# Seven block products for the first layer of both halves of a second MLP, with its last weights converted early and parked in DRAM

## The chip, the cores and the metric

One core of one Trainium2 chip runs the whole program in one launch. The metric is the device time of an execution in microseconds (us), from runs on the chip. Engine names are those of the profile: PE is the matrix engine (PEld its weight loads), DVE the vector engine, ACT the scalar engine, POOL the GpSimd engine, SP the engine whose queue issues nearly all DMAs.

## What is computed

Attention with rotary positions over 4 x 8 heads of 576 tokens, then two MLPs over the 2304 tokens of width 512, each with 2048 hidden features. Cut to what matters here:

```python
x = attention(q, k, v)                 # 2304 tokens x 512
h = x @ moe_w_in                       # 512 -> 2048
g = where(h >= 1, h, where(h <= -1, 0, (h + 1) ** 2 / 4))
x = g @ moe_w_out                      # 2048 -> 512
h = x @ moe2_w_in                      # second MLP, first layer
g = s * max(h, 0) ** 2 + b
out = g @ moe2_w_out                   # second MLP, second layer
```

## The kernel before

**Number format.** Every operand of the MLP products is a pair of float32r parts, high and low, and a product is three matmuls: high by high, high by low, low by high. A *slice* is 128 hidden features: its 128 x 512 columns of the first layer and of the second one, both parts, in one SBUF tile of 128 x 2 x 1024. Each MLP has 16 slices, used as two sets of eight: set_a and set_b for the first MLP, set_c and set_d for the second. The weights come in as 64-bit numbers. `Slice.convert` (L116 to L135) makes the two parts of half a slice from a raw tile `wraw` of 512 KB: two ACT passes (L128, L133), four DVE passes (L129 to L132) and four POOL pieces (through `pool_tt`, L92). There are two `wraw` buffers (`RB`), and one each of the scratch tiles `wa` and `wm` per scratch pool (`WB`). `Slice.half` (L142) converts into the slice's tile, or, where the half was parked, only loads it back (L148). `Slice.park` (L152) converts in place in `wraw` and writes the result to DRAM (L161).

**Attention.** 16 pairs of heads, nine units each, 144 units in all (loop at L595). A unit gets its score matmuls (L341), a maximum on DVE (L343), an exponential on ACT (L348), transposes, and a share of first-MLP work as filler (`beside`, L443; 1440 tokens, set_a). `do_load` hangs conversions and parks on units: `PARK_AT` (L56) parks eight halves, those of every second slice of set_b, at units 96, 102, ..., 138.

**Stages.** After it come, in this order:

| stage | tokens | weights | chunks | conversions beside it |
|---|---|---|---|---|
| a (L915) | 1440 to 2304 | set_a | 3 of 288 | set_b: 8 converted, 8 loaded from the park |
| b (L916) | 0 to 1440 | set_b | 352, 368, 352, 368 | set_c, 16 halves over b and c |
| c (L917) | 1440 to 2304 | set_b | 2 of 432 | the rest of set_c |
| d (L920) | 0 to 2304 | set_c | 448, then 4 of 464 | set_d, 16 halves |
| last (`seven`, L706) | 0 to 2304 | set_d | 384, then 4 of 480 | none |

Stages a to d run in `stage` (L622). A step is one chunk by one slice: 12 matmuls of the first layer into one PSUM bank (`hps`, L172), the activation on ACT and DVE, and three steps later (`GL`) the 12 second-layer matmuls (L684 to L686) into four PSUM banks that add up over the eight slices. With the eighth slice a bank is read out and written to DRAM (L691 to L695): stage d writes partial sums `zd`, to which the last stage adds its own.

**The last stage.** Its first chunk runs as in `stage`. From the second chunk on, two slices and a chunk of 480 make a 2 x 2 block product (two slices, two halves of the width, two halves of the chunk). `product` (L806) runs on seven products of sums of blocks instead of eight products of blocks: 7 x 6 matmuls of 240 columns (L813) where the plain form has 24 matmuls of 480. The sums of weight blocks are made in `sums` (L737) once for a pair of slices, the sums of token blocks in `token_sums` (L775) once for a chunk; DVE puts the seven results together from PSUM (L880 to L887). Second-layer matmuls are those of L726 to L728, in the plain form, through a queue `late` of products still due.

**What sets the order.** From stage a on the PE's order is written by hand, as the program emits it. The order on the other engines and on SP's queue, and all of the attention's, is made by a planner from simulated times; `issue_after` only gives an instruction an earliest place. SP's queue runs in order.

## Time and profile before

| | us |
|---|---|
| median of 3 runs | 1132.64 |
| lowest and highest run | 1129.21, 1133.21 |
| the profiled execution | 1131.69 |
| its span, first to last instruction | 1129.9 |
| PE busy | 1081.4 (96%) |
| DVE, ACT, POOL busy | 700.3, 672.1, 508.3 |
| end of attention's units, about | 430 |
| stage d, first matmul to the last stage's first | 732.99 to 933.59 |
| last stage, first to last matmul's start | 933.59 to 1125.47 |

A row of windows gives each engine's busy time in a stretch; where PE's busy time equals the stretch, the PE never waited. In a timeline row the first number is the start from the beginning of the span, the second the time from there to the end of the row's last instruction. Neighbouring matmuls overlap in the pipeline, so the price of a matmul in a dense stream is the distance between two starts, not its own duration.

### The profile page before, as it was taken

To read this page: it belongs to the slowest core of one execution; us is meant where nothing else is said; L and a number is where in the kernel's file an instruction comes from. 1 tells how busy PE (TensorE), PEld (TensorE's weight loads), DVE (VectorE), ACT (ScalarE), POOL (GpSimd) and SP (SyncE) were. 2 spreads that over 40 slices of the span, in tenths; PEclk is the share of its full clock that TensorE was granted. 3 is DMA by queue.
4 is the path that set the end of the run, shared out by engine and by line. 5 is a ranking of instruction groups with operands and counts; after the bars stand their busy time and mean duration, and the time that the engine had idled before them with its cause. 6 is when DMAs were issued, how large, how long until landed. Compare 5 with 4: busy or idle time off the path is not lost.

```text
span 1129.9 us, 19370 instructions
## 1 busy us (share of the span) xinstructions
PE 1081.4 (96%) x7008; PEld 981.4 (87%) x7008; DVE 700.3 (62%) x1223; ACT 672.1 (59%) x1472; POOL 508.3 (45%) x676
## 2 busy tenths in 40 slices
PE   3999989889999999999999999999999999999998
PEld 3666678778898989999999999999888889999997
DVE  6888898787675763554555645443334386667754
ACT  4777777666676765565544544477667668334421
POOL 7969887876572332355555634425444240000000
PEclk9999999999999999999999999999999999999999
DMA  7565756545555432445344543223233303221210
GB/s 225 161 177 167 202 150 177 166 134 155 172 177 161 122 128 75 152 140 173 114 152 131 153 125 109 93 65 122 72 98 111 104 20 106 81 71 53 80 61 36
DMA packets 89760, 140.51 MB, mean 124 GB/s; under 512 B 28864, under 2 KB 66752, under 8 KB 89664
## 3 DMA queue, kind: packets, MB, share of 16 engines
q1 hardware_dynamic: 89664, 139.27, 40.8%
q8 instruction: 55, 0.90, 0.3%
q14 instruction: 41, 0.34, 0.1%
HBM read 95.22 MB, written 30.74 MB: 111 GB/s over the span
## 4 chain that ended last, share of the span: by engine, by line
PE 76%; DVE 7%; DMA 4%; POOL 4%; ACT 3%; issue 2%; SPq 1%; POOLq 0%; ACTq 0%; DVEq 0%
PE hps L172 23%; PE yps L684 7%; PE yps L686 7%; PE yps L685 7%; PE sum L813 7%; PE sc L341 4%; PE h L172 3%; PE av L389 3%; PE yps L728 3%; PE yps L727 3%; PE yps L726 3%; PE y L172 3%; PE tp L363 2%; POOL kin L92 2%; DVE nm L343 2%
## 5 line engine op out<-in xcount | busy, mean ns | idle before, releaser
L172 PE MATMUL hps<-xh,w 128*128 128x464 f32 (+6 forms) x960 | 263.2, 340 | 0.0
L92 POOL TENSOR_TENSOR wm<-wm,w 128x256 f32<-128x256 f32 x112 | 101.2, 924 | 210.1 <-ACT w L133 172.3
L172 PEld LDWEIGHTS hps<-xh,w 128*128 128x128 f32 x960 | 173.4, 188 | 7.9
L172 PE MATMUL hps<-xl,w 128*128 128x464 f32 (+6 forms) x480 | 162.6, 339 | 0.0
L684 PE MATMUL yps<-gh,w 128*128 128x464 f32 (+5 forms) x448 | 152.2, 340 | 0.5 <-ACT ys L466 0.5
L685 PE MATMUL yps<-gl,w 128*128 128x464 f32 (+5 forms) x448 | 152.1, 339 | 0.0
L686 PE MATMUL yps<-gh,w 128*128 128x464 f32 (+5 forms) x448 | 152.1, 339 | 0.0
L341 PE MATMUL sc<-kh,qs 128*128 128x288 f32 x336 | 103.4, 330 | 32.5 <-ACT p L348 20.8
L343 DVE TENSOR_REDUCE nm<-sc 128x1 f32<-128x576 f32 x144 | 107.6, 751 | 40.6 <-PE sc L341 39.8
L92 POOL TENSOR_TENSOR xl<-xs,xh 128x288 fp32r<-128x288 f32 (+5 forms) x132 | 96.6, 758 | 70.7 <-ACT xh L98 70.6
L348 ACT ACTIVATE p<-sc,nm 128x576 f32<-128x576 f32 x144 | 106.6, 743 | 33.3 <-DVE nm L343 32.6
L341 PEld LDWEIGHTS sc<-kh,qs 128*128 128x128 f32 x336 | 64.9, 196 | 50.0 <-ACT p L348 28.9
L102 DVE TENSOR_TENSOR gl<-ar,gh 128x464 fp32r<-128x464 f32 (+2 forms) x48 | 36.4, 757 | 113.2 <-ACT gh L98 113.2
L102 DVE TENSOR_TENSOR gl<-ac,gh 128x288 fp32r<-128x288 f32 (+3 forms) x112 | 71.9, 643 | 40.6 <-ACT gh L98 40.1
L363 PE MATMUL tp<-ident,p 128*128 128x128 f32 x576 | 89.6, 280 | 6.1 <-ACT p L348 3.3
L341 PE MATMUL sc<-kz,qs 128*128 128x288 f32 x336 | 95.0, 302 | 0.0
L172 PEld LDWEIGHTS hps<-xl,w 128*128 128x128 f32 x480 | 90.1, 188 | 4.0
L195 DVE SCALAR_TENSOR_TENSOR ac<-hps,ac 128x288 f32<-128x288 f32 (+3 forms) x72 | 37.6, 523 | 84.8 <-ACT ac L194 84.4
L92 POOL TENSOR_TENSOR w<-wm,wa 128x256 fp32r<-128x256 f32 x112 | 88.5, 808 | 0.2
L684 PEld LDWEIGHTS yps<-gh,w 128*128 128x128 f32 x448 | 84.1, 188 | 4.6 <-ACT ys L466 0.8
L686 PEld LDWEIGHTS yps<-gh,w 128*128 128x128 f32 x448 | 84.2, 188 | 3.8
L685 PEld LDWEIGHTS yps<-gl,w 128*128 128x128 f32 x448 | 84.1, 188 | 3.9
(143 smaller groups left out, 2548.3 us busy)
## 6 DMA issues: line engine op xcount, KB each, us to landing
wraw<-in_ww SPq DMA_DIRECT2D x64, 512.0 KB, 4.0
kin<-in_k SPq DMA_DIRECT2D x15, 576.0 KB, 4.9
qin<-in_q SPq DMA_DIRECT2D x15, 576.0 KB, 3.9
kh<-kin SPq DMA_DIRECT2D x60, 144.0 KB, 2.6
xs<-xd SPq DMA_DIRECT2D x44, 144.0 KB, 2.4
yd<-ys SPq DMA_DIRECT2D x40, 144.0 KB, 2.7
xd<-u SPq DMA_DIRECT2D x16, 288.0 KB, 2.4
kz<-kin SPq DMA_DIRECT2D x30, 144.0 KB, 2.6
```

Of the source, the lines that this page charges most:

```text
L92: nc.gpsimd.tensor_tensor(out=out[c], in0=in0[c], in1=in1[c], op=op)
L102: tt(out=dst_lo, in0=src, in1=dst_hi, op=ALU.subtract)
L172: m = nc.tensor.matmul(out_ps, l, r, start=(i == 0), stop=(i == n - 1))
L195: nc.vector.scalar_tensor_tensor(out=c, in0=h, scalar=1.0, in1=c, op0=ALU.max, op1=ALU.min)
L341: nc.tensor.matmul(sc[:, half, o:o + n], l, r[:, k0:k0 + n], start=m == 0, stop=m == len(todo) - 1)
L343: maxs[i * 9 + k] = nc.vector.tensor_reduce(out=nm, in_=sc[:, :, :288], axis=AX.XY, op=ALU.max, negate=True).ins
L348: exps[i * 9 + k] = nc.scalar.activation(p, sc[:, :, :288], AF.Exp, bias=nm, scale=1.0, accum_out=sums_t[i][:, col:col + 1]).ins
L363: m = nc.tensor.transpose(v[:, c, :], p[:, c * P:(c + 1) * P], ident)
L684: nc.tensor.matmul(acc, wh, gh, start=f == 0, stop=False)
L685: nc.tensor.matmul(acc, wh, gl, start=False, stop=False)
L686: nc.tensor.matmul(acc, wl, gh, start=False, stop=last)
L813: nc.tensor.matmul(acc, l, r, start=j == 0, stop=j == len(t) - 1)
```

## The change

Stage d takes the form of the last stage: `seven` becomes three functions (`front`, `main`, `ask`) and is made twice, for set_c (result to `zd`, nothing added, so PSUM is read out by ACT) and for set_d (as before). Since the conversions of set_d had lain in stage d, all 16 are moved ahead and parked: four halves at attention units (which now carry twelve parks: six apart up to unit 120, then three apart), five in stage a, seven in stages b and c (`mix` places them among the other conversions). During the last chunk of the new stage d `beside_c` loads all 16 back, splits the next stage's first tokens and makes its first weight sums. The slices' tiles are named apart ("w" and "x") so that each new use waits for a given old one. Products of the second layer that are still due pass from one stage to the next through one common `late`.

The diff, without its re-indented loop and the declarations:

```diff
-PARK_AT = range(96, 144, 6)
+PARK_AT = [*range(96, 120, 6), *range(120, 144, 3)]
...
+    parkd2 = dram.tile([NF - GA, 2, P, 2, 512], F32, name="parkd2")
...
-    parking = [sl for sl in set_b[::2] for _ in range(2)]
+    set_d = [Slice(None, ww2, f, ROOMS[f - GA - GA // 2], parkd2) for f in range(GA, NF)]
+    parking = [sl for sl in set_b[::2] + set_d[:2] for _ in range(2)]
...
+    laid = set(set_d)
     def convert():
         while pending:
             sl = pending.pop(0)
+            if sl in laid:
+                sl.park(wst, scratch)
+                break
             if sl.made < 2:
                 sl.half(wst, scratch)
                 break
...
                 if last:
-                    y = to.pop((c, d))
-                    nc.vector.tensor_tensor(out=y, in0=acc, in1=y, op=ALU.add)
+                    if part is None:
+                        y = q2.tile([P, n], F32, tag="yo", name="yo", bufs=YB)
+                        nc.scalar.copy(y, acc)
+                    else:
+                        y = to.pop((c, d))
+                        nc.vector.tensor_tensor(out=y, in0=acc, in1=y, op=ALU.add)
...
+        def ask(k, pool=qx, tag="xs", bufs=XB):
             n0, n = chunks[0]
+            raws[0, k] = pool.tile([P, n], F32, tag=tag, name="xs2", bufs=bufs)
+            nc.sync.dma_start(out=raws[0, k], in_=src[k, :, n0:n0 + n])
...
-    stage(xd, a, yd[0], [], set_a, act1, set_b, halves / (GA * len(a)))
-    stage(xd, b, y1d, [yd[g] for g in range(GA // G1)], set_b, act1, set_c, halves / (GA * len(b + c)))
-    stage(xd, c, y1d, [yd[0]], set_b, act1, [], halves / (GA * len(b + c)))
-    end = seven(y1d, e, out, zd, set_d)
-    stage(y1d, d, zd, [], set_c, act2, set_d, halves / (GA * len(d) - 6), next(end))
...
+    front_c, main_c, _ = seven(y1d, e, zd, None, set_c, qx_tiles, room_c, spread_c)
+    front_d, main_d, ask_d = seven(y1d, e, out, zd, set_d, first_d, room_d, spread_d)
+
+    def beside_c(q, mark):
+        if q == 0:
+            for k in range(3):
+                ask_d(k)
+            ask_d(3, scratch[0], "wm", WB)
+        for f in ((0, 1, 2), (3, 4), (5, 6), (7,))[q]:
+            for _ in range(2):
+                set_d[f].half(wst, scratch)
+        for k in ((), (), (0, 1, 2, 3), (4, 6))[q]:
+            front_d(k, mark)
+
+    def mix(one, two):
+        both = []
+        for i, sl in enumerate(one):
+            both += [sl] + two[i * len(two) // len(one):(i + 1) * len(two) // len(one)]
+        return both
+
+    twice = lambda sls: [sl for sl in sls for _ in range(2)]
+    left = twice(set_d[2:])
+    stage(xd, a, yd[0], [], set_a, act1, mix(twice(set_b), left[:5]), 21 / (GA * len(a)))
+    stage(xd, b, y1d, [yd[g] for g in range(GA // G1)], set_b, act1, mix(left[5:], twice(set_c)), 15 / (GA * len(b)))
+    stage(xd, c, y1d, [yd[0]], set_b, act1, [], 0.8, lambda i, mark: front_c(i + GA - 1, mark))
+    main_c(beside_c)
+    main_d(lambda q, mark: None)
+    with tc.high_priority(P2):
+        while late:
+            second()
```

## Rows read from the trace of the kernel before

**Rows 1.** The page's first part: busy time, share of the span, instructions.

```profile
PE 1081.4 (96%) x7008; PEld 981.4 (87%) x7008; DVE 700.3 (62%) x1223; ACT 672.1 (59%) x1472; POOL 508.3 (45%) x676
```

**Rows 2.** PE's waits from 440 us on: total us, times, longest.

```profile
PE yps L684 <- ACT ys L466: 0.5, 1, 0.5
```

**Rows 3.** Windows: stretch, length, busy PE, PEld, DVE, ACT, POOL, clock, DMA.

```profile
200.00:240.00 40.00, 35.88 (x265) 30.74 (x263) 30.76 (x49) 24.86 (x60) 32.59 (x42) 0.96 0.54 154
...
272.00:310.00 38.00, 37.78 (x300) 33.99 (x296) 27.79 (x52) 26.86 (x69) 21.01 (x31) 1.00 0.54 161
...
350.00:430.00 80.00, 78.12 (x618) 70.36 (x618) 53.02 (x103) 56.88 (x145) 21.82 (x34) 1.00 0.38 118
...
461.00:537.00 76.00, 75.47 (x562) 75.23 (x561) 38.59 (x70) 43.44 (x103) 36.83 (x48) 1.00 0.51 164
537.00:660.00 123.00, 123.00 (x753) 122.92 (x752) 70.11 (x119) 61.76 (x129) 74.46 (x104) 1.00 0.47 140
660.00:733.00 73.00, 73.00 (x376) 70.09 (x375) 35.43 (x59) 35.42 (x66) 27.82 (x36) 1.00 0.31 96
...
840.00:933.60 93.60, 93.60 (x447) 83.52 (x447) 51.34 (x81) 62.73 (x108) 35.33 (x42) 1.00 0.25 80
933.60:962.90 29.30, 29.30 (x170) 29.30 (x169) 17.15 (x41) 23.36 (x52) 0.00 (x0) 1.00 0.31 99
...
1041.00:1081.00 40.00, 40.00 (x269) 37.32 (x268) 27.11 (x54) 15.18 (x34) 0.00 (x0) 1.00 0.19 56
```

**Rows 4.** Timeline of PE: first matmul of stage d, of the last stage, last one.

```profile
732.99 0.36 PE L172 MATMUL hps<-xh,w 128*128 128x448 f32 x1
...
933.59 0.33 PE L172 MATMUL hps<-xh,w 128*128 128x384 f32 x1
...
1125.47 0.38 PE L728 MATMUL yps<-gh,w 128*128 128x480 f32 x1
```

**Rows 5.** Timeline of one pair of slices: 42 product matmuls, then 24 second-layer ones.

```profile
1080.71 0.95 PE L813 MATMUL sum<-xh,w 128*128 128x240 f32 x7
...
1085.43 0.38 PE L726 MATMUL yps<-gh,w 128*128 128x480 f32 x1
...
1090.43 0.38 PE L728 MATMUL yps<-gh,w 128*128 128x480 f32 x1
```

**Rows 6.** Instructions on the tiles wraw and wm: ns min/median/max, first and last start.

```profile
L128 ACT ACTIVATE wa<-wraw x64: 654/671/711, 59.6 to 921.3; 128x512 f32<-128x512 f32 x64
L129 DVE TENSOR_SCALAR wm<-wa x64: 414/428/1102, 60.3 to 922.0; 128x512 uint32<-128x512 uint32 x64
L130 DVE SCALAR_TENSOR_TENSOR wm<-wa,wm x64: 659/693/1290, 62.5 to 922.4; 128x512 uint32<-128x512 uint32 x64
L131 DVE TENSOR_SCALAR wa<-wm x64: 397/428/1020, 64.5 to 923.2; 128x512 uint32<-128x512 uint32 x64
L132 DVE SCALAR_TENSOR_TENSOR wa<-wraw,wa x64: 674/693/1276, 68.3 to 923.6; 128x512 f32<-128x512 uint16 x64
L133 ACT CAST w<-wm x56: 602/621/627, 63.2 to 923.2; 128x512 fp32r<-128x512 f32 x56
L92 POOL TENSOR_TENSOR wm<-wm,w x112: 723/924/1282, 70.3 to 924.9; 128x256 f32<-128x256 f32 x112
L92 POOL TENSOR_TENSOR w<-wm,wa x112: 717/737/1279, 73.6 to 926.6; 128x256 fp32r<-128x256 f32 x112
```

**Rows 7.** The page's DMA issues: size of one, median us to landing.

```profile
wraw<-in_ww SPq DMA_DIRECT2D x64, 512.0 KB, 4.0
```

**Rows 8.** Instructions on the tile parkd: the park writes.

```profile
L161 SPq DMA_DIRECT2D parkd<-wraw x8: 319/325/326, 277.4 to 413.2; - x8
```

**Rows 9.** Timeline of PE: waits at the score matmuls after two parks.

```profile
355.08 0.40 PE L341 MATMUL sc<-kh,qs 128*128 128x288 f32 x1 [0.78 <-ACT p L348]
...
411.97 0.40 PE L341 MATMUL sc<-kh,qs 128*128 128x288 f32 x1 [0.78 <-ACT p L348]
```

**Rows 10.** Waits of SP's queue, 330 to 440 us.

```profile
SPq L139 <- DMA parkd<-wraw: 10.4, 5, 2.3
```

202 lines of the change are left out of this document (113 added, 89 removed).

## The prediction

> **What bounds the kernel now.** I read the page's busy shares first [rows 1]: the PE is busy 96% of the span, every other engine at most 62%. An average can hide stages, so the PE's waits came next. From 440 us to the end there is one wait, of 0.5 us [rows 2]; the windows say the same stage by stage: in stages b, c and d and in the last stage PE busy equals the length of the stretch, while DVE is at 49 to 68% and POOL at 0 to 61% [rows 3]. In the attention the picture changes on the way: 4.1 us of 40 idle at 200 to 240 us, 0.2 of 38 at 272 to 310, 1.9 of 80 at 350 to 430 [rows 3]. So from about 270 us on the end is set by the length of the PE's stream: a shorter stream pays in full as long as no new wait appears, and a new wait on the PE costs in full. The granted clock is 1.00 in all these rows but the first (the 2.4 GHz level), so it plays no part.
>
> **The new stage d.** Its price can be read without any model, since the last stage is the same work in the new form: 2304 tokens, eight slices, chunks of 384 and four of 480. Stage d runs from 732.99 to 933.59, 200.6 us. The last stage runs from 933.59 to one matmul after 1125.47, that is 1125.7: 192.1 us [rows 4]. Both streams are dense, so the swap removes 200.6 - 192.1 = 8.5 us. Does it add up from single matmuls? In one pair the 42 product matmuls take 1085.43 - 1080.71 = 4.72 us, 0.112 each; the second-layer ones are 1090.43 - 1085.43 over 23 distances, 0.217 each [rows 5]. A plain first layer would take 24 x 0.217 = 5.2 us, so a pair saves 0.5 us, and 16 pairs 7.8; the rest comes from the chunk sizes (1248 matmuls instead of 960, but fewer columns in all). I take the 8.5 of the whole stage, with 7 to 9 as bounds.
>
> The two forms differ in two places. The new stage d adds nothing to its results: ACT reads PSUM out instead of DVE. That takes 20 additions off DVE and gives ACT 20 copies, where ACT is at 15 of 40 us [rows 3]: nothing on the path, since at a chunk's end the next use of those banks comes behind 42 product matmuls, 4.7 us. And beside its last chunk it has loads and sums for the next stage, below.
>
> Of TensorE's price for narrow matmuls a rule speaks against this change. By the Trainium skill, TensorE: Matmul & The Clock Gate, section Back-to-back issue gap, streams of load-and-multiply pairs were measured at about 81 ns for 128 columns and 131 ns for 512. An estimate from that page by a straight line is 96 ns at 240 columns and 127 at 480; more and narrower matmuls would then be the dearer form. This trace does not agree: 0.112 and 0.217 us [rows 5] are nearly in proportion to the columns, though the weight loads fill 37.3 of 40 us [rows 3].
>
> **The conversions moved ahead.** One conversion costs ACT 0.67 + 0.62 = 1.3 us, DVE 0.43 + 0.69 + 0.43 + 0.69 = 2.2, POOL 2 x 0.92 + 2 x 0.74 = 3.3 [rows 6], and as a park one more DMA of 512 KB out and later one in. Sixteen leave stage d: there they were hidden, so their removal gains nothing. Where do they go?
>
> *Attention, units 120 to 141: four more.* Parks are 3.2 us per unit apart in units (277.4 to 413.2 us for 42 units [rows 8]), so the stretch is 350 to 430 us. DVE goes from 53.0 to 62 of 80 us, ACT from 56.9 to 62, POOL from 21.8 to 35 [rows 3, 6]: room in the mean. A local price shows: the 1.9 us that the PE idles there stand at two places, with a wait of 0.78 us each for an exponential [rows 9]; they belong to the parks at units 120 and 138, both the fourth unit of a pair of heads (where the pair's normalization also wants DVE and ACT), while the parks at 126 and 132 cost nothing. The new list has three such units, 120, 129 and 138: one more, 1.9 / 2 = 0.9 us. Bounds: zero (at 272 to 310 us conversions and parks lie even closer, and the PE idles 0.2 us [rows 3]) and four times 0.9 = 3.8 us. I take 0.9, the row of the same stretch.
> On SP's queue each park is followed by a raw load that waits for the write to land, up to 2.3 us, five times so far at 330 to 440 us [rows 10]; behind it stand loads of K, Q and V and writes of first-MLP results. Four more such waits are 9 us of queue in 80; they are in the bounds.
>
> *Stage a: five more* (21 items in 24 steps instead of 16). DVE goes from 38.6 to 50 of 76 us, ACT from 43.4 to 50, POOL from 36.8 to 53 [rows 3, 6]. Scarcest are the two raw buffers: a conversion holds one for the load, 4.0 [rows 7], and until DVE's last pass, 2.9; a park for 4.0, a chain of 5.7 and the landing, 2.3, 12 us in all. That is 8 x 6.9 + 5 x 12 = 115 of 2 x 76 us. It fits, at zero; if it slips, set_b's later halves come late, but stage b wants a new slice only every 24 matmuls, 3.9 us.
>
> *Stages b and c: five and two more.* DVE 70 to 81 of 123, POOL 74 to 91; in c DVE gets two conversions, the token splits and two weight sums that stage d had, some 15 us on 35 of 73 [rows 3, 6]. The tight spot is the chunk's end: DVE must read out the first PSUM bank within 21 matmuls of 0.163 us, 3.4 us; one pass of a conversion holds it for 0.7, at worst 1.3 [rows 6]. Zero, with 2 us as upper bound for all three stages.
>
> **The seam.** The 16 loads, 8.4 MB, may start with the last chunk of the new stage d, four pairs of 9.9 us; the next stage then wants a slice every 24 matmuls, 4.1 us (29.3 us for 170 [rows 3]), the last one 68 us after the start. At stage a's 164 GB/s [rows 3] the loads take 51 us; the DMA engines were then half busy, so it may be half of that. SP issues them behind the token loads; what waits for them is DVE, whose weight sums at the fourth pair need slices loaded at the first. Zero, and no gain: the old seam had no wait either [rows 2].
>
> **Sum.** Against the profiled execution, 1131.69 (span 1129.9 and 1.8 around it): 1131.69 - 8.5 + 0.9 = 1124.1. The median of the runs is 0.95 above that execution, so I predict 1125.0. With the bounds (7 to 9 gained, 0 to 5.8 lost) and the runs' own spread of 4 us between lowest and highest, this case's range is 1121 to 1129.
>
> **Rivals.**
> *The parks stall the attention.* For it: maxima and exponentials stand behind conversions on DVE and ACT in order, and at 200 to 240 us the PE idled 10.3%. Against it: 272 to 310 us. At that share the 80 us lose 8.2 instead of 1.9, 6.3 more: 1129.5 by the profiled execution.
> *The conversions become late work in stages a to c.* For it: raw buffers three quarters taken, POOL at 70% and more. Against it: stage b without a wait at 0.33 conversions a step. If the next chunk's token split falls behind a conversion's POOL work, each of two or three chunk starts waits 3.3 us, 7 to 10 in all: 1130 to 1133.
> *Slower: the parked weights come late at the seam.* If SP's queue holds them back until the next stage starts, eight slices of 1.05 MB at 164 GB/s take 6.4 us each, where the PE needs 4.1: 4.0 + 8 x 6.4 - 33 = 22 us of waits, 1146. By the 51 and 68 us above, 17 us of delay cost nothing; the change is slower than before from a delay of about 25 us on. Against it: the rooms of the first eight halves are free when the chunk begins.
> *Slower: price by the matmul, not by the column.* If the new stage's 288 additional matmuls cost as in stage d while the columns saved gave back little, it would lose; half of 288 x 0.209 less 8.5 is 22 us, 1154. The Trainium skill's rule above would make it some 15 us slower, an estimate from that page. The last stage's own 192.1 us speak against both.
>
> **How the numbers follow.** Forecast 0.70, parks 0.14, stages a to c 0.09, late weights 0.05, price by the matmul 0.01, something else 0.01. About 0.5%, 5.7 us, is what a measurement of this kernel can tell from no change: faster means below 1127.0. The forecast gives 0.62 of that (of its 0.70 a part lies above), and the milder ends of the parks and stages rivals 0.05: 0.67. Slower by over 0.5% is most of the late weights and the price: 0.05. Within: 0.28. For 8 in 10 the range goes from 1121 to 1130: nearly all of the forecast and the milder half of the first two rivals.
>
> **What would show it.** Right: the PE dense from 440 us to the end, the new stage d 192 us long, set_d's loads landed before the last chunk's fourth pair, about three waits of 0.8 us at 350 to 430 us, conversions in stages a to c with no wait of the PE behind them. Wrong: attention units that end over 3 us later; a PE wait for DVE at chunk ends of stages a to c; a wait for a set_d tile; a new stage d that differs from the last stage by over 1 us.

## The result, and the profile of the changed kernel

The changed kernel takes 1148.05 us in the median (1144.69 to 1149.86, four runs), the kernel before 1132.93 beside it (1129.21 to 1133.53): a ratio of 1.0137, with a 95% interval of 1.0105 to 1.0169. It is slower by 1.4%, where I had forecast 1125.0 and a range of 1121 to 1130. The profiled execution took 1149.86, with a span of 1148.1 (before 1129.9).

The page's first part of the changed kernel, to be held against [rows 1]:

```profile
PE 1084.5 (94%) x7296; PEld 989.7 (86%) x7296; DVE 799.1 (70%) x1443; ACT 643.8 (56%) x1472; POOL 484.4 (42%) x636
```

PE is busy for 3.1 us more, but the span grew by 18.2. No engine but the PE is near its limit in the mean. Where the time went is seen stage by stage. Windows of the changed kernel (columns as in [rows 3]):

```profile
350.00:430.00 80.00, 77.52 (x605) 69.54 (x606) 62.14 (x117) 59.66 (x150) 34.28 (x50) 1.00 0.51 164
461.00:540.00 79.00, 75.41 (x558) 74.08 (x557) 47.56 (x86) 44.53 (x107) 45.33 (x55) 1.00 0.53 181
540.00:680.00 140.00, 130.08 (x770) 128.28 (x768) 88.89 (x144) 71.57 (x150) 102.41 (x137) 0.98 0.57 178
680.00:759.00 79.00, 77.07 (x385) 72.79 (x385) 61.57 (x108) 38.21 (x72) 32.40 (x38) 0.98 0.38 122
759.00:951.00 192.00, 192.00 (x1251) 181.10 (x1250) 120.86 (x248) 90.42 (x196) 0.00 (x0) 1.00 0.28 93
951.00:1144.00 193.00, 193.00 (x1251) 181.36 (x1249) 129.68 (x262) 81.37 (x177) 0.00 (x0) 1.00 0.22 67
```

The last two lines are the new stage d and the last stage: both dense, both of the same length. Lines two to four are stages a, b and c: the PE stands idle for 3.6, 9.9 and 1.9 us, where [rows 3] has 0.5, 0 and 0. PE's timeline of the changed kernel gives the boundaries that answer to [rows 4]:

```profile
759.43 0.34 PE L174 MATMUL hps<-xh,w 128*128 128x384 f32 x1
...
946.65 2.26 PE L174 MATMUL hps<-wf,w 128*128 128x384 f32 x12
...
1143.81 0.38 PE L744 MATMUL yps<-gh,w 128*128 128x480 f32 x1
```

From the first matmul of stage d to one matmul past the last start it is now 1143.81 + 0.22 - 759.43 = 384.6 us; before it was 392.7. So the new form gives 8.1 us. The lengths of the other stages, from first matmul to first matmul: attention and what precedes it 450.7 (before 447.5), a 89.4 (85.0), b 140.2 (125.3), c 79.1 (75.1). That is 3.2 + 4.4 + 14.9 + 4.0 = 26.5 us lost against 8.1 won. Their difference, 18.4, is the longer span but for 0.2.

PE's waits from 450 us to the end, which answer to the single line of [rows 2]:

```profile
PE yps L692 <- DVE yp L699: 11.1, 7, 4.4
PE yps L693 <- DVE gl L103: 1.4, 2, 0.9
PE yps L692 <- ACT yo L702: 1.4, 1, 1.4
PE yps L692 <- ACT ac L196: 0.6, 1, 0.6
PE yps L692 <- ACT ys L470: 0.5, 1, 0.5
...
```

The first line is the largest: seven waits at ends of chunks, four in stage b and three in stage c, where DVE reads out a PSUM bank (L699) that the next chunk's second layer (L692) wants. Stage a has none of them: beside the 0.5 us that stood there before, its waits are for a copy of ACT (L702) and for activations, 3.1 us in pieces of 1.4 and less. The largest wait, 4.39 us, can be followed back. PE, DVE, ACT and SP around it, from the timelines of the changed kernel (brackets: the wait just before, and what ended it):

```profile
583.33 0.40 PE L692 MATMUL yps<-gh,w 128*128 128x368 f32 x1 [4.39 <-DVE yp L699]
...
579.11 0.43 DVE L131 TENSOR_SCALAR wm<-wa 128x512 uint32<-128x512 uint32 x1 [3.47 <-ACT wa L130]
579.57 0.69 DVE L132 SCALAR_TENSOR_TENSOR wm<-wa,wm 128x512 uint32<-128x512 uint32 x1
...
581.08 0.69 DVE L134 SCALAR_TENSOR_TENSOR wa<-wraw,wa 128x512 f32<-128x512 uint16 x1
581.69 1.06 DVE L103 TENSOR_TENSOR gl<-ac,gh 128x368 fp32r<-128x368 f32 x1
582.67 0.94 DVE L699 TENSOR_TENSOR yp<-yps,yp 128x352 f32<-128x352 f32 x2
...
578.41 0.66 ACT L130 ACTIVATE wa<-wraw 128x512 f32<-128x512 f32 x1 [3.35 <-DMA wraw<-in_ww]
...
580.82 0.49 ACT L99 CAST gh<-ac 128x368 fp32r<-128x368 f32 x1
...
569.76 0.32 SPq L163 DMA_DIRECT2D parkd<-wraw  x1
571.00 2.16 SPq L645 DMA_DIRECT2D xs<-xd  x2
573.26 0.38 SPq L141 DMA_DIRECT2D wraw<-in_ww  x1
```

And the waits of SP's queue from 565 to 576 us:

```profile
SPq L163 <- POOL wraw L93: 3.2, 1, 3.2
SPq L645 <- POOL xl L93: 3.1, 3, 1.4
```

Read it from below. SP's queue stands 3.2 us for POOL's pieces of a park, until the park's write leaves at 569.76. The park holds one of the two raw buffers until this write has landed (the 24 park writes took 2.6 us in the median, which makes it about 572.4). By then the queue stands at two token loads (L645), which wait for POOL's token splits, and POOL makes these behind the park's pieces. The next raw load is issued at 573.26, and ACT's first pass (L130) stands until 578.41 for it. DVE's first pass (L131) stands 3.47 us for ACT. In DVE's order the PSUM read-out L699 stands behind that pass and the three that follow, though the PE had filled its bank by 577. L103 between them was late in a second way: its operand `gh` is made by ACT only at 580.82 (L99), and ACT had itself stood behind L130 until 578.41. L699 comes at 582.67, and the PE, which has waited since 578.94, goes on at 583.33. In stages a to c, DVE stood 56.2 us for conversions that had not got their data; before the change 0.5. The waits of DVE at 447 to 733 us before the change, then at 450 to 760 after it (total, times, longest):

```profile
DVE wm L129 <- ACT wa L128: 0.5, 1, 0.5
```

```profile
DVE wm L131 <- ACT wa L130: 56.2, 25, 5.7
```

And what ACT's first pass waited for in the same stretch of the changed kernel, none of which stands in ACT's list before:

```profile
ACT wa L130 <- DMA wraw<-in_ww: 29.4, 17, 3.7
...
ACT wa L130 <- POOL wraw L93: 11.9, 6, 4.4
ACT wa L130 <- POOL w L93: 8.1, 2, 5.6
```

So two things come late: raw data (and the buffer for it), and POOL's pieces, which hold the scratch tiles. The experiments take them apart.

### The profile page after: what moved, and what is told of

The parts are those of the page before. It is cut to its first block, busy times and chain, and to the rows that moved or that the text cites. A ratio compares the mean times of both kernels' runs of the same rounds, so it can differ in the third digit from the quotient of the medians.

```text
span 1148.1 us, 20174 instructions
## 1 busy us (share of the span) xinstructions
PE 1084.5 (94%) x7296; PEld 989.7 (86%) x7296; DVE 799.1 (70%) x1443; ACT 643.8 (56%) x1472; POOL 484.4 (42%) x636
## 4 chain that ended last, share of the span: by engine, by line
PE 47%; DMA 6%; DVE 4%; POOL 3%; ACT 2%; issue 2%; SPq 0%; POOLq 0%; ACTq 0%; DVEq 0%
PE sum L828 13%; PE hps L174 8%; PE yps L744 6%; PE yps L743 6%; PE yps L742 6%; DMA wraw<-in_ww 4%; PE yps L692 2%; PE yps L693 2%; PE yps L694 2%; PE y L174 1%; PE h L174 1%; DMA yp<-yd 1%; POOL wm L93 1%; ACT wa L130 1%; DVE wm L132 1%
## 5 line engine op out<-in xcount | busy, mean ns | idle before, releaser
L174 PE MATMUL hps<-xh,w 128*128 128x288 f32 (+4 forms) x640 | 165.4, 326 | 0.0
L744 PE MATMUL yps<-gh,w 128*128 128x480 f32 (+1 forms) x320 | 118.5, 370 | 0.0
L742 PE MATMUL yps<-gh,w 128*128 128x480 f32 (+1 forms) x320 | 118.4, 370 | 0.0
L743 PE MATMUL yps<-gl,w 128*128 128x480 f32 (+1 forms) x320 | 118.4, 370 | 0.0
L174 PEld LDWEIGHTS hps<-xh,w 128*128 128x128 f32 x640 | 114.8, 190 | 1.1
L692 PE MATMUL yps<-gh,w 128*128 128x288 f32 (+3 forms) x288 | 95.2, 331 | 14.1 <-DVE yp L699 11.1
L174 PE MATMUL hps<-xl,w 128*128 128x288 f32 (+4 forms) x320 | 104.3, 326 | 0.0
L103 DVE TENSOR_TENSOR gl<-ac,gh 128x288 fp32r<-128x288 f32 (+3 forms) x112 | 74.9, 670 | 31.2 <-ACT gh L99 29.9
L693 PE MATMUL yps<-gl,w 128*128 128x288 f32 (+3 forms) x288 | 94.3, 327 | 1.4 <-DVE gl L103 1.4
L93 POOL TENSOR_TENSOR xl<-xs,xh 128x288 fp32r<-128x288 f32 (+3 forms) x92 | 75.6, 843 | 45.1 <-ACT xh L99 45.1
L694 PE MATMUL yps<-gh,w 128*128 128x288 f32 (+3 forms) x288 | 94.0, 326 | 0.0
L367 PEld LDWEIGHTS tp<-ident,p 128*128 128x128 f32 x576 | 72.4, 145 | 9.2 <-ACT p L352 3.7
L131 DVE TENSOR_SCALAR wm<-wa 128x512 uint32<-128x512 uint32 x64 | 34.9, 545 | 63.2 <-ACT wa L130 62.6
L99 ACT CAST gh<-ac 128x288 fp32r<-128x288 f32 (+3 forms) x112 | 52.0, 466 | 46.9 <-DVE ac L197 46.6
```

The lines of the kernel that those rows point to most:

```text
L93: nc.gpsimd.tensor_tensor(out=out[c], in0=in0[c], in1=in1[c], op=op)
L174: m = nc.tensor.matmul(out_ps, l, r, start=(i == 0), stop=(i == n - 1))
L367: m = nc.tensor.transpose(v[:, c, :], p[:, c * P:(c + 1) * P], ident)
L692: nc.tensor.matmul(acc, wh, gh, start=f == 0, stop=False)
L693: nc.tensor.matmul(acc, wh, gl, start=False, stop=False)
L694: nc.tensor.matmul(acc, wl, gh, start=False, stop=last)
```

## The experiments

e1, e2, e5, e6, e11 and e13 differ from the changed kernel in the twelve parks of stages a to c alone; e3, e12, e14, e17 and e18 choose the scratch tiles of the attention's parks anew too, e4 and e7 touch the stages' result tiles, e14 the loads of the stages' other conversions, and e8 to e10 and e15 to e18 move parks. Stage lengths are those of each profiled execution, from first matmul to first matmul; "d to end" is from the first matmul of stage d to the end of the span. Ratios are to the kernel before, which had medians of 1130.7 to 1132.2 us beside these runs and 1132.93 beside the changed kernel; so a difference of two medians can be off by some 2 us, and the ratios and the stage lengths say which ones hold. Each edit also gives the planner a new problem, so the order on ACT, DVE, POOL and SP differs from run to run.

Six runs came out inside one of the ranges expected (e3, e5, e7, e10, e14, e18); e6, e11, e12 and e15 fell between two, e1, e2 and e13 within 1.2 us of one, and e4, e8, e9, e16 and e17 above all of theirs.

| kernel | median us | ratio (95%) | a starts | a | b | c | d to end |
|---|---|---|---|---|---|---|---|
| before | 1132.93 | | 447.5 | 85.0 | 125.3 | 75.1 | 396.9 |
| changed | 1148.05 | 1.0137 (1.0105 to 1.0169) | 450.7 | 89.4 | 140.2 | 79.1 | 388.7 |
| e1_noparks | 1123.82 | 0.9941 (0.9920 to 0.9962) | 447.7 | 85.4 | 125.3 | 75.1 | 389.2 |
| e2_nowrite | 1144.52 | 1.0119 (1.0081 to 1.0158) | 451.7 | 90.4 | 136.2 | 80.4 | 388.4 |
| e3_scratch | 1146.09 | 1.0124 (1.0089 to 1.0158) | 449.9 | 90.5 | 139.3 | 76.1 | 388.7 |
| e4_raw3 | 1166.66 | 1.0313 (1.0275 to 1.0352) | 448.6 | 88.1 | 156.7 | 83.5 | 388.7 |
| e5_staged | 1144.59 | 1.0106 (1.0076 to 1.0137) | 453.2 | 91.6 | 131.3 | 77.7 | 388.6 |
| e6_nopool | 1135.16 | 1.0031 (1.0016 to 1.0047) | 448.7 | 88.8 | 129.8 | 77.8 | 388.4 |
| e7_yq4 | 1162.91 | 1.0284 (1.0257 to 1.0311) | 448.2 | 89.2 | 152.7 | 83.1 | 388.7 |
| e8_attn24 | 1144.89 | 1.0126 (1.0097 to 1.0155) | 456.0 | 94.6 | 125.3 | 76.6 | 388.6 |
| e9_inD12 | 1150.21 | 1.0146 (1.0115 to 1.0178) | 451.0 | 85.0 | 125.4 | 77.0 | 411.4 |
| e10_inD8 | 1132.38 | 1.0004 (0.9986 to 1.0023) | 455.5 | 85.0 | 125.4 | 76.8 | 390.6 |
| e11_static | 1136.27 | 1.0034 (1.0016 to 1.0052) | 448.0 | 90.5 | 128.6 | 78.0 | 388.6 |
| e12_static_scratch | 1131.09 | 1.0003 (0.9987 to 1.0019) | 449.6 | 88.4 | 127.2 | 75.6 | 388.6 |
| e13_static_nopool | 1123.24 | 0.9932 (0.9908 to 0.9955) | 449.4 | 85.4 | 125.6 | 75.1 | 388.4 |
| e14_ahead | 1143.27 | 1.0114 (1.0083 to 1.0144) | 450.3 | 88.9 | 137.1 | 81.1 | 388.7 |
| e15_inD10 | 1132.56 | 1.0006 (0.9991 to 1.0021) | 448.3 | 85.4 | 126.4 | 75.1 | 394.3 |
| e16_inD8_a4 | 1132.29 | 1.0002 (0.9989 to 1.0015) | 449.7 | 91.5 | 127.3 | 75.1 | 388.7 |
| e17_inD8_a4s | 1130.28 | 0.9985 (0.9966 to 1.0005) | 448.6 | 91.4 | 125.4 | 75.1 | 388.6 |
| e18_spread | 1125.50 | 0.9944 (0.9924 to 0.9964) | 452.2 | 85.4 | 125.4 | 75.1 | 389.1 |

### Is it the parks of stages a to c? (e1)

My theory after the result: the whole loss in a to c comes from the twelve parks there. The rival: something else that the change brought (twelve parks in the attention, the new stage's token splits in stage c, the shared tiles) does it.

```diff
-                sl.park(wst, scratch)
+                sl.parked.append(parkd[0, len(sl.parked)])
```

> The changed kernel without its twelve parks in stages a to c (the four in the attention stay); the six slices of set_d concerned are loaded at the seam from what set_b parked, so their conversion is left out and every load stays. The changed kernel took 1148.1 us, the one before 1132.9. Theory 1: the whole loss lies in those parks. Then stages a to c run without a wait of the PE, and the time is 1132.9 - 8.3 (the new stage d as its trace shows it) + 0 to 2 (attention) = 1125 to 1127. Theory 2: something else of the change (rooms, order of the queues, front of the new stage) makes the waits at the chunk ends: then it stays above 1140.

Measured: 1123.82 us, 24.2 below the changed kernel (22 by the two ratios, 23 by the lengths of a, b and c), with a, b and c at 85.4, 125.3 and 75.1, within 0.4 us of their lengths before the change. All that is left of PE's waits from 450 us on is the one of [rows 2]:

```profile
PE yps L692 <- ACT ys L470: 0.5, 1, 0.5
```

So the parks cost 22 to 24 us, and the rest of the change, the new form with its seam and the attention's four parks, does what was forecast for the whole: 1123.82 against 1125.0.

### What of a park? (e2 to e7, e11 to e14)

A park holds ACT for two passes, DVE for four and POOL for four pieces; it holds a raw buffer from load to landing; it has a load and a write. Each of these runs takes away one or two of them.

**The write alone.** The park makes everything and writes nothing.

```diff
+            self.parked.append(self.parks[self.f - GA, n] if out else parkd[0, n])
+            if out:
+                nc.sync.dma_start(out=self.parked[n], in_=parts.bitcast(F32))
```

> The changed kernel with its twelve parks in stages a to c converting as before but not written to DRAM (the loads at the seam take what set_b parked, so the result of these six slices is left out). Theory A, the two raw buffers are held too long: a park holds one for 9.7 us instead of 12, so a part comes back, 1138 to 1144. Theory B, the write's wait on SP's queue (for POOL, and then of the next raw load for its landing) holds up the loads behind it: nearly all comes back, 1126 to 1131. Theory C, the engines' work for 12 conversions is too much in these stages: nothing, 1146 to 1150.

Measured: 1144.52, 3.5 us below the changed kernel, 2 by the ratios, whose intervals overlap; b is 4.0 shorter, a and c together 2.3 longer. The landing isn't the main part.

**The scratch pool.** The line that picks one of two scratch pools counts `made`, which stays 0 while a slice is parked: all parks shared one pool. Here they alternate.

```diff
-            pool = pools[self.f * 2 + self.made & 1 if len(pools) > 1 else 0]
+            pool = pools[(self.made or len(self.parked)) & 1 if len(pools) > 1 else 0]
```

> The changed kernel with the parks taking turns between the two scratch pools for wa and wm; so far they all use the first one, and ACT's first pass waited 20 us in 8 waits for POOL to release it, beside 29 us in 17 waits for the raw load. Theory D, the one scratch pool makes the chain late: 20/49 of the 23 us lost come back, 1137 to 1141. Theory A (raw buffers): 1145 to 1150. Theory C (engines' work): 1146 to 1150.

Measured: 1146.09, 2 us below, which the intervals don't tell apart. Alone, while raw data still come late, it gives nothing that shows.

**A third raw buffer.** The parks get a raw buffer of their own; its room comes from the result tiles of the stages (four instead of five).

```diff
+YQ = 4
-            raw = stage.tile([P, HW], self.ww.dtype, tag="wraw", name="wraw", bufs=RB)
+            raw = stage.tile([P, HW], self.ww.dtype, tag="wraw", name="wraw", bufs=RB if stage is wst else 1)
-                sl.park(wst, scratch)
+                sl.park(wst3, scratch)
-                yp = q2.tile([P, n], F32, tag="yo", name="yp", bufs=YB)
+                yp = q2.tile([P, n], F32, tag="yo", name="yp", bufs=YQ)
```

> The changed kernel with a third raw buffer that the parks of stages a to c alone use; to make room the buffers of partial results in those stages are four instead of five, which works against it. Theory A, the raw buffers: the raw loads come in time, ACT's waits for them go from 29 us to under 10, and at least half of the 23 us comes back, 1126 to 1137. Theory B (SP's queue): a little, 1143 to 1148, since the writes stay. Theory C or D: 1145 to 1150.

Measured: 1166.66, worse by 18.6, with b at 156.7. That says nothing of the raw buffer until the missing fifth result tile is measured alone.

**Four result tiles alone.**

```diff
+YQ = 4
-                yp = q2.tile([P, n], F32, tag="yo", name="yp", bufs=YB)
+                yp = q2.tile([P, n], F32, tag="yo", name="yp", bufs=YQ)
```

> The changed kernel with four instead of five buffers of partial results in stages a to c, as in the run with the third raw buffer, and nothing else. If these buffers caused that run's 1167, it takes 1160 to 1170, and the third raw buffer by itself gave nothing or little. If it takes 1146 to 1152, the third buffer itself made it slower, by letting parks crowd together.

Measured: 1162.91. One result tile less costs 14.9 us, b 152.7. PE waits of it at 450 to 780 us:

```profile
PE yps L693 <- DVE yp L700: 20.9, 8, 5.5
```

The wait for the read-out, 11.1 us in the changed kernel, has grown to 20.9 with one tile less to read out to; why wasn't followed further. Against e7, the third raw buffer gives a 1.1 us shorter stage a and a 4.0 longer stage b: nothing gained, though ACT's waits for raw data in a to c are 16.5 us with it and 24.2 without. While result tiles are short, these two runs can't say what a third raw buffer is worth.

**Results off the raw buffer.** The parks write their parts to an idle slice tile of the next set, so that the raw buffer is free after DVE's last pass, as in an ordinary conversion.

```diff
+            if spare:
+                parts = spare.pop(0)
...
+    spares(wpb, 4)
     stage(xd, a, ...)
+    spares(wpa, 7)
     stage(xd, b, ...)
```

> The changed kernel in which eleven of the twelve parks of stages a to c put their result into a weight room that is not in use yet, instead of back into the raw buffer. The raw buffer is then free after DVE's last pass (6.9 us instead of 12) and no raw load waits for a write to land. Theory A, raw buffers: most of the 23 us comes back, 1125 to 1135. Theory F, any late raw load stands in front of ACT and DVE in their planned order, whoever holds the buffer, and the twelve more loads and chains are what there is too much of: a small part, 1140 to 1147. Theory C2, POOL is the scarce engine: 1145 to 1150.

Measured: 1144.59; b falls by 8.9 of its 14.9, to 131.3. But in the profiled execution a starts 2.5 later and is 2.2 longer, and the median gains only 3.5. Giving the buffer back earlier takes back the larger part of stage b's loss, and this way out costs elsewhere.

**Neither raw load nor raw buffer.** The parks convert the same raw tile, loaded once into an idle slice tile.

```diff
-            raw = self.load(stage, n * HW)
-            parts = raw.bitcast(F32R).rearrange("p (t n) -> p t n", t=2)
+            if spare:
+                raw, parts = spare.pop(0)
+            else:
+                raw = self.load(stage, n * HW)
+                parts = raw.bitcast(F32R).rearrange("p (t n) -> p t n", t=2)
```

> The changed kernel in which eleven of the twelve parks of stages a to c convert one raw tile that is loaded once for a stage, in a weight room not in use yet, and put the result beside it (so these halves of set_d hold other weights than they should). ACT, DVE and POOL do the same work and all writes stay; no raw buffer is held and no raw load awaited by these parks. Theory A or F with the raw load as the late part: most of the 23 us comes back, 1125 to 1133. Theory G, the engines' chains themselves stand in the way in the in-order queues, whenever the raw data comes: 1137 to 1146.

Measured: 1136.27, 11.8 below the changed kernel, b at 128.6. PE's wait for DVE's read-out from 450 us on has fallen from 11.1 us to this:

```profile
PE yps L703 <- DVE yp L710: 2.2, 5, 1.3
```

**No POOL pieces.** The parks keep ACT's and DVE's passes, the raw buffer and the write (the high part twice); POOL does nothing for them.

```diff
+            if not pieces:
+                return
             pool_tt(out=m, in0=m, in1=hi, op=ALU.subtract)
             pool_tt(out=lo, in0=m, in1=a, op=ALU.add)
```

> The changed kernel with its twelve parks in stages a to c without their POOL pieces, 40 us of POOL work (the low parts of these weights are left out; the high part is written out twice, in two DMAs of 256 KB). ACT, DVE, raw loads and writes stay. Theory C2, POOL is the scarce engine: most comes back, 1125 to 1133. Theory A or F: the chain is 3.3 us shorter, so a part, 1138 to 1145.

Measured: 1135.16, 12.9 below; b at 129.8. So taking POOL's pieces away gives as much as taking the raw loads away. It isn't POOL's work alone: by the edit a park also gives its raw buffer back earlier, and ACT's waits for raw data fall from 29.4 to 19.9 us.

**Both.** e11 and e6 together.

> The run with the static raw tile, and in addition the parks without their POOL pieces (the low parts of these weights are left out, and eleven halves hold other weights). ACT's and DVE's passes and all writes stay. If the raw data (12 us) and POOL (13 us) are the two halves of the loss: 1124 to 1128. If ACT's and DVE's passes cost by themselves: 1130 to 1135.

Measured: 1123.24, 24.8 below the changed kernel and the same as with no park at all (1123.82). The edit is e11's and e6's, nothing else. Here ACT and DVE still make all twelve times six passes and SP writes all twelve halves, each in two DMAs, and the stages are as long as before the change; PE's waits are again the single 0.5 us. This is the run that settles it: **the parks' own passes on DVE and ACT cost nothing; the loss is what raw data and POOL's chain make late.** The two medians add up (11.8 + 12.9 is 24.7), but they aren't two halves of one loss. By the table, either run alone takes back 10 to 12 of stage b's 14.9 us and at most 1.9 of the 8.4 us of a and c; only both together take back nearly all of both. In stage b either alone gives most of it, in a and c only both do.

Could it be the new order instead? At the ends of chunks it isn't. At each of stage b's four chunk ends as many conversion passes stand just ahead of the first read-out in e13 as in the changed kernel (four, three, three, four). At the first one, to be held against the rows around 4.39 us above (the read-out is L717 here):

```profile
567.63 0.43 DVE L131 TENSOR_SCALAR wm<-wa 128x512 uint32<-128x512 uint32 x1
...
569.61 0.69 DVE L134 SCALAR_TENSOR_TENSOR wa<-spare,wa 128x512 f32<-128x512 uint16 x1
570.42 1.00 DVE L717 TENSOR_TENSOR yp<-yps,yp 128x352 f32<-128x352 f32 x2
```

The same passes in the same place, but the first does not wait, and neither does the PE. DVE's waits for ACT's first pass at 450 to 760 us are these, against 56.2 in the changed kernel; the PE feels none of them:

```profile
DVE wm L131 <- ACT wa L130: 15.3, 8, 5.8
```

**Alternating scratch, with static raw data.** e11 with e3's line.

> The run with the static raw tile (1136.3; eleven parks convert one raw tile, so these halves hold other weights), and the parks take turns between the two scratch pools. Half two is the scratch pool: the rest comes back, 1124 to 1129. Half two is POOL's work, or the passes' places in the in-order queues: 1133 to 1138.

Measured: 1131.09, 5.2 below e11. The same line that gave at most 2 us alone gives 5 once the raw data are there (5.9 by the stages; by the ratios 3.5, where the intervals just overlap). So of what is lost with the raw data there, some 5 us go with the one scratch pool that all parks shared, and some 8 stay until POOL's pieces go (e13), 3.3 us a park at the durations of [rows 6] on an engine that had 74.5 of 123 us full.

**Mending the chain where it lies.** e5's rooms, e3's line, and each raw load issued one conversion ahead of its use.

```diff
+            def rest():
+                self.convert(raw, pools, parts[:, 0], parts[:, 1])
+                self.parked.append(self.parks[self.f - GA, n])
+                nc.sync.dma_start(out=self.parked[n], in_=parts.bitcast(F32))
+            if ahead is None:
+                rest()
+            else:
+                ahead.append(rest)
```

> The changed kernel with the parks where they are and the whole computation done: results put into weight rooms not in use yet, the two scratch pools in turn, and in stages a to c each raw load issued one conversion ahead of its passes. If late raw data and the scratch pool in front of ACT and DVE make the loss: 1126 to 1134. If the passes and POOL's work are too much there: 1138 to 1146.

Measured: 1143.27, b at 137.1. It gains 4.8 us, 2.6 by the ratios, and the intervals overlap. By its edit each load also holds one of the two raw buffers for longer; whether that is what remains wasn't taken apart. It was not enough.

### Where is there room? (e8 to e10, e15 to e18)

These runs make all sixteen parks, in other places, to see how many a stage takes free. That a stage takes a few free and then turns dear would follow from a lack of engine time as well as from lateness; e13 tells the two apart for ACT and DVE, not for POOL, whose pieces it leaves out.

**All in the attention.** 24 parks, two units apart, none asked for behind.

```diff
-PARK_AT = [*range(96, 120, 6), *range(120, 144, 3)]
+PARK_AT = range(96, 144, 2)
-    parking = [sl for sl in set_b[::2] + set_d[:2] for _ in range(2)]
+    parking = [sl for sl in set_b[::2] + set_d for _ in range(2)]
```

> The changed kernel with all 16 halves of set_d parked in the attention: 24 parks, one every two units from unit 96 on, none in stages a to c, which convert as before the change. Theory 1 (the loss is where the parks lie): stages a to c dense as without parks, d and last stage 389 us, so 1123.8 plus what eight more parks cost the attention. If they cost there what the first four did, 0.2 to 1 us: 1124 to 1127. If 12 us a park on two raw buffers (one per 6 us, and parks come every 6.5) is too much: the attention is late by 8 us and more, 1132 to 1140.

Measured: 1144.89. Stage b is at its 125.3 again; a starts at 456.0 and takes 94.6. Against the kernel before that is 8.5 + 9.6 us. The attention has no room for all sixteen either: six of the 24 park writes leave only in stage a, at 467 to 512 us, and a's waits of the PE, 6.0 us from 472 to 549, are in the main for ACT's copies.

**In stage d, twelve.** The parks for set_d are made beside the new stage d itself, between its block products, with a raw buffer of their own.

```diff
+    slots = {(0, 1): 1, (0, 6): 0, (0, 7): 1, **{(c, q): s for c in (1, 2, 3) for q, s in ((0, 1), (2, 0), (3, 1))}}
+    def more_c(c, q):
+        if (c, q) in slots:
+            left.pop(0).park(wst3, [scratch[slots[c, q]]])
...
-    main_c(beside_c)
+        main_c(beside_c, more_c)
```

> The changed kernel with the twelve parks taken from stages a to c into the new stage d itself, where POOL is idle and DVE busy 65%: three in its first chunk, three in each of the next three, with a raw buffer of their own (the buffers of results there are three instead of five). If the loss belongs to stages a to c and their tight chunk ends: stages a to c as before the change, d a little longer, 1124 to 1129. If any conversion beside a dense PE stalls it: 1132 to 1145.

Measured: 1150.21. Stages a and b are back at 85.0 and 125.4; from d to the end it takes 22.7 more. PE's waits from 450 us on have two new heads, the operands that ACT makes for the block products:

```profile
PE sum L829 <- ACT xl L100: 8.5, 1, 8.5
PE sum L829 <- ACT wt L100: 4.1, 1, 4.1
```

**In stage d, eight,** and eight of set_d in the attention (16 parks there, three units apart).

```diff
+PARK_AT = range(96, 144, 3)
+    slots = {(0, 1): 1, (0, 7): 1, **{(c, q): s for c in (1, 2, 3) for q, s in ((0, 1), (3, 1))}}
```

> As the run before, but 16 parks in the attention (eight for set_d, one every three units from unit 96 on) and only eight in the new stage d, at pairs where no token sums are made. Without parks in stages a to c: 1124 to 1128 if four more parks cost the attention 0 to 2 us, as the first four did; 1129 to 1136 if they crowd it as 24 did.

Measured: 1132.38, no change against before. From d to the end 390.6, near the 388.7 without a park there; a starts at 455.5 instead.

**Ten in d, two in a; eight in d, four in a.** The attention has its four of set_d in both.

```diff
-    stage(xd, a, ..., mix(twice(set_b), left[:5]), 21 / (GA * len(a)))
+    stage(xd, a, ..., mix(twice(set_b), left[:2]), 18 / (GA * len(a)))     # e15, and e10's slots with (4, 0) and (4, 1)
+    stage(xd, a, ..., mix(twice(set_b), left[:4]), 20 / (GA * len(a)))     # e16, with e10's slots
```

> The changed kernel with twelve parks in the attention as changed, two in stage a, none in b and c, and ten in the new stage d, at places where no token sums are made (eight there cost 1.9 us in the run with sixteen parks in the attention, twelve cost 22). 1123.8 without parks, plus 2 to 3 in stage d, 1 to 2 in stage a, 0 to 2 in the attention: 1127 to 1131. If the two added parks in the last chunk hold up the loads of set_d: 1134 to 1142.

> The whole computation: twelve parks in the attention as changed, four in stage a, none in b and c, eight in the new stage d at places without token sums. 1123.8 without parks, plus 1.9 in stage d, plus 0 to 3.5 in stage a (two cost 0, five cost 4.4), plus 0 to 2 in the attention: 1126 to 1130, under the kernel before by 2 to 6 us.

Measured: 1132.56 and 1132.29. In e15, two parks in a leave it at 85.4 and ten in d make it 394.3, 5.6 us more than without. In e16, eight in d cost nothing (388.7) and four in a make it 91.5, 6.5 more than before. Nearly all of this is one wait and what came behind it. PE's waits, ACT's pass in front of the copy L703 that the PE wanted, and a window around both (columns as in [rows 3]):

```profile
PE yps L693 <- ACT yo L703: 3.6, 1, 3.6
...
516.20 0.66 ACT L131 ACTIVATE wa<-wraw 128x512 f32<-128x512 f32 x1 [2.62 <-DMA wraw<-in_ww]
...
510.00:525.00 15.00, 11.44 (x69) 11.20 (x68) 9.17 (x18) 7.63 (x19) 9.91 (x13) 0.77 0.80 265
```

It is the same thing on ACT: the copy stands behind a pass that waits for raw data. The granted clock is 0.77 over these 15 us, which is 3.4 us more (0.23 x 15); with the 3.6 that is 7.0, half a microsecond over the 6.5. In the changed kernel no wait in stage a is longer than 1.4 us and the clock is 1.00 throughout, so its five parks, of which three were written there as in e16, cost less, 4.4.

**The same with alternating scratch** (e3's line added to e16).

> The same, with the parks of stage a taking turns between the two scratch pools (worth 2 to 5 us of twelve parks in two earlier runs): 0 to 2 us less than the run before it, 1125 to 1129.

Measured: 1130.28, which the intervals don't tell from e16. b falls by 1.9 us to 125.4, a stays at 91.4.

**Spread: two in a, two in b, eight in d, four in the attention.**

```diff
-    stage(xd, a, ..., mix(twice(set_b), left[:5]), 21 / (GA * len(a)))
-    stage(xd, b, ..., mix(left[5:], twice(set_c)), 15 / (GA * len(b)))
+    stage(xd, a, ..., mix(twice(set_b), left[:2]), 18 / (GA * len(a)))
+    stage(xd, b, ..., mix(left[2:4], twice(set_c)), 12 / (GA * len(b)))
...
+    left = left[4:]
+    slots = {(0, 1): 1, (0, 7): 1, **{(c, q): s for c in (1, 2, 3) for q, s in ((0, 1), (3, 1))}}
```

> The whole computation: twelve parks in the attention as changed, two in stage a, two in stage b (twelve conversions there instead of fifteen as changed, ten before), eight in the new stage d, the two scratch pools in turn. Stage a 85.4, stage c 75.1, stage d and the last one 388.7 as measured with these numbers; stage b 125.3 if two parks fit, up to 131 if a chunk end waits once or twice: 1124 to 1130.

Measured: 1125.50 us (1123.41 to 1128.83), a ratio of 0.9944 (0.9924 to 0.9964) to the kernel before. It is the whole of the change with its parks elsewhere and e3's line in it, 22.5 us faster than the changed kernel and faster than the kernel before by 0.6%. Its windows over stages a, b and c, columns as above:

```profile
452.50:537.50 85.00, 84.37 (x633) 83.92 (x632) 53.78 (x93) 52.46 (x129) 44.65 (x55) 1.00 0.49 161
538.00:663.00 125.00, 125.00 (x768) 125.00 (x767) 79.16 (x127) 67.68 (x140) 90.39 (x120) 1.00 0.54 164
663.00:738.00 75.00, 75.00 (x385) 72.05 (x384) 57.25 (x99) 36.22 (x68) 24.31 (x28) 1.00 0.30 94
```

Compare its stage b with that of the changed kernel: POOL is busy for 90.4 of 125 us here and 102.4 of 140 there, 72 and 73%; DVE for 63% in both. One has no wait, the other 9.9 us of them. The shares can't tell the two apart, in part because the waits themselves stretch the stage: the changed kernel's 102.4 us of POOL work would be 82% of a stage of 125. DVE's waits for late conversions in stages a to c say more: 56.2 us in the changed kernel, and here

```profile
DVE wm L132 <- ACT wa L131: 7.0, 4, 4.3
```

But their sum isn't the price either: e13 has 15.3 us of them and loses nothing, e11 28.3 and has b at 128.6, e14 28.9 and has b at 137.1. So it matters as well what stands behind the waiting pass. In e18 the last three instructions ahead of the first read-out hold no pass at three of stage b's four chunk ends, and DVE waits there for the PE; how much of its gain is this order and how much the smaller number of parks wasn't taken apart.

## Why the prediction was wrong, step by step

**The new stage d: right.** 8.5 us forecast, with 7 to 9 as bounds, 8.1 measured; dense, with no wait. The rival that prices by the matmul falls with it.

**The seam: right, though not by the sign that I gave.** No PE wait names a tile of set_d, so the rival of late weights falls. But the loads had not all landed by the last chunk's fourth pair: that pair starts at 926.75, and two loads are issued behind 940.9. The next stage starts at 946.65 and wants the last slice some 29 us later (seven slices of 4.1 us), which is why nobody waited.

**Attention: near the forecast, by one execution of the kernel before.** Two waits for an exponential at 350 to 450 us, 1.9 us in all, where [rows 9] had two and I expected three. The idle time of the PE at 350 to 430 went from 1.9 to 2.5 us. The stage behind starts 3.2 us later, which is past my sign of 3. But 2.1 of these are there before any changed park: the 553rd score matmul, of a unit just ahead of the first one, starts at 351.10 before and 353.22 after. From there to stage a it is 96.4 us before and 97.5 after, and 97.3 to 98.4 in the seventeen kernels with these twelve parks. So the four parks cost 0.9 to 2.0 us, 1.1 in the changed kernel, where I had taken 0.9. SP's queue did what I worked out: nine waits of a raw load for a park's write, 19.0 us, where [rows 10] had five with 10.4:

```profile
SPq L141 <- DMA parkd<-wraw: 19.0, 9, 3.7
```

**Stages a to c: the step that failed.** "It fits, at zero" for stage a, and "Zero, with 2 us as upper bound for all three stages": measured 23.3 us by stages (4.4 + 14.9 + 4.0), 22 to 24 by e1. I had seen the right place ("the tight spot is the chunk's end") and the right resource (raw buffers three quarters taken), and then put a wrong price on it: "one pass of a conversion holds it for 0.7, at worst 1.3". That is the pass's own duration. In the changed kernel's trace a pass holds DVE from the moment at which all before it is done, also while its operand is missing; that is the operand's lateness plus the passes, up to 5.7 us and 2.2, where 3.4 us was all that I had found the chunk's end to allow. On ACT it is the same, as e16's stage a shows. e13 shows the other side: with the data there and no POOL chain, the same passes in the same places at stage b's chunk ends cost nothing. The hold of a raw buffer until the write has landed I had only as a mean of buffer time, and POOL's pieces only as POOL's busy time; that both make the next operand late stood nowhere in the sum.

One more term was too small, without harm: I put DVE's work in stage c at some 15 us on 35, and it is 61.6 of 79. In e1 it is 57.1 of 75.2, and the PE waits for none of it.

The second half of the error is the sum of buffer time, 115 of 152 us, by which I let it fit (against the 85.0 us that stage a lasts it is 115 of 170). Such a mean left no slack for an instruction whose place in the order is fixed ahead: without raw loads (e11) or with the buffers given back earlier (e5), 11.6 and 8.9 of stage b's 14.9 us came back, and in e16 even four parks in stage a cost 6.5 us, with a sum of 8 x 6.9 + 4 x 12 = 103. Nor did the parks stay where I had counted them: of the five in stage a two were written only in b, which had seven.

**The rival named the place but not the mechanism.** "The conversions become late work in stages a to c" put three waits of 3.3 us on chunk starts, for a token split behind POOL's work. Of the listed waits the largest were at chunk ends and for DVE; the loss was 22 to 24 us and not 7 to 10; I had given it 9 in 100. A token split behind POOL's pieces does stand in the chain of the 4.39 us, but as a delay of a raw load. And the long waits were followed by slow matmuls, which no part of the sum had. Windows around the 4.39 us wait (PE busy first, the clock in the last column but two):

```profile
575.00:583.00 8.00, 3.94 (x25) 3.64 (x23) 4.37 (x8) 3.50 (x8) 5.48 (x8) 1.00 0.55 175
583.00:586.00 3.00, 2.67 (x10) 2.66 (x11) 2.46 (x7) 1.24 (x3) 1.72 (x3) 0.66 0.87 325
586.00:588.00 2.00, 2.00 (x10) 2.00 (x10) 1.95 (x5) 1.28 (x3) 0.00 (x0) 0.66 0.46 120
588.00:590.00 2.00, 2.00 (x14) 2.00 (x13) 2.00 (x5) 1.12 (x2) 1.30 (x2) 1.00 0.82 257
```

The granted clock is 0.66 in the two windows behind the wait, in part the lower of the two levels (1.2 and 2.4 GHz), and 1.00 again from 588; at 584.17 to 587.24 neighbouring matmuls start 0.31 us apart, where 583.57 to 583.91 it is 0.17. The other long wait of stage b, 3.84 us at 654.18, looks alike: the clock is 0.72 from 654 to 660. In stage b the PE's idle time is 9.9 of the 14.9 us lost, and a granted clock of 0.98 over 140 us accounts for some 3 more; in stage c 0.98 over 79 us makes 1.6 beside 1.9 of waits. The last 2 us of b, and as much in a and c together, are not placed; the page itself says that a busy PE need not be one at its peak.

**What stays open.** How the 8 us that e12 leaves over e13 divide: in the one chain followed above POOL's pieces held up the park's write, and with it the raw buffer, and the token splits behind them; the other waits weren't followed so far. Whether POOL's pieces are late there or POOL has too little time isn't told apart. Why stage b gains most of its loss from either remedy alone, and a and c only from both. And how much the planner's new order does in the runs that move parks (e8 to e10, e15 to e18).

## What to carry to other kernels

Background work that an engine takes in order is priced by how late its operands are and by what stands behind it, not by what its passes take: before moving such work, ask of each of its buffers who frees it and when, and which instruction of the main line stands behind the first one that waits. Engine shares read from the slowed stage don't answer that (POOL at 72% without a wait, at 73% with 10 us of them). In this kernel room came in small portions, and spreading the work was what paid: asked for as two parks in stage a, two in b and eight in d they were free (with two scratch pools in turn; by the trace one was written in a and three in b), where five asked for in a and five in b cost 19 us.

## What the runs showed of the hardware

The pass that reads raw data on DVE (two inputs in SBUF) got longer where more POOL work lay beside it. Groups of instructions in stage b of the changed kernel and, without POOL's pieces, of e13 (count, then busy us and mean ns); before the change it took 740 ns:

```profile
L134 DVE SCALAR_TENSOR_TENSOR wa<-wraw,wa 128x512 f32<-128x512 uint16 x17 | 15.0, 887 | 0.4
L132 DVE SCALAR_TENSOR_TENSOR wm<-wa,wm 128x512 uint32<-128x512 uint32 x17 | 13.6, 802 | 0.5
```

```profile
L132 DVE SCALAR_TENSOR_TENSOR wm<-wa,wm 128x512 uint32<-128x512 uint32 x16 | 12.7, 792 | 0.5
...
L134 DVE SCALAR_TENSOR_TENSOR wa<-wraw,wa 128x512 f32<-128x512 uint16 x11 | 8.3, 752 | 0.3
```

By the Trainium skill, SBUF — State Buffer, section SBUF: two separate sides, a DVE instruction with two inputs in SBUF and a GpSimd instruction that reads SBUF share a pair of ports that the first to start holds to its end. The trace agrees in part: one such pass goes from 740 to 887 and back to 752 ns (five more in e13, which read the fixed raw tile, take 795), the other stays at 793, 802 and 792. Either way it is some 0.15 x 17 = 2.5 us of DVE in stage b, beside 30 us in which DVE stood for late conversions, so it isn't what made the kernel slower.

The lower clock behind a wait was the other thing: a wait of 4.4 us was followed by a granted clock of 0.66 from 583 to 588, by which 0.34 x 5 = 1.7 us are lost, over a third of the wait itself again. The loss did not follow the length of the wait: in e6 it came behind a wait of 2.0 us (at 578.32) and is as large, 0.30 x 5.6 = 1.7, and in e16 it was 3.4 behind one of 3.6. Behind the 1.35 us of the changed kernel's stage a (at 518.14) the clock stayed at 1.00. The window in e6:

```profile
578.40:584.00 5.60, 5.60 (x25) 5.60 (x26) 5.31 (x11) 3.08 (x6) 1.32 (x2) 0.70 0.89 291
```
